# Partial sums added in memory by transfers, roundings held on ScalarE, a half chunk's work moved: an attention and two-FFN kernel

## The chip, the cores and the metric

The kernel runs on one core of one Trainium2 chip. The time is that of one execution on the device, in microseconds. The kernel before took 1273.68 us, the median of 3 runs (1272.46 to 1275.25). Engines are named as the profile does: PE is TensorE's matmuls, PEld its weight loads, DVE VectorE, ACT ScalarE, POOL GpSimd, SP SyncE, which here issues most transfers.

## The reference

```python
# x [8, 8, 512, 64], state [8, 8, 32, 64]
a     = softmax(scale * x @ state^T)          # tokens read the state
xread = a @ state
a2    = softmax(scale * state @ x^T)          # the state reads the tokens
sread = a2 @ x
x = concat([xread, sread], axis=2)            # -> [4352, 512]: 8 x (512 + 32) rows
x = relu(x @ w_in) ** 2 @ w_out               # w_in [512, 2048], w_out [2048, 512]
out = ((x @ w1) * (x @ w2) @ w3) @ w_out2     # w1, w2 [512, 1024], w3 [1024, 1024], w_out2 [1024, 512]
```

All in float32.

## The kernel before

Tokens are worked in nine chunks: chunks 0 to 7 are the 512 token rows of each batch, and chunk 8 (`B` in the code) holds the 256 rows of all state reads; it is called the half chunk here. A float32 matmul is done in three passes of a rounded part and a rest: `split` (lines 80 to 85) rounds a tile on ScalarE (line 84) and takes the rest by a subtraction on VectorE (line 85).

**First phase** (to 674.9 us): attention and the first FFN. Chunks 0, 1 and 2 start before all weights are converted, so their FFN sums are closed in parts: three for chunks 0 and 1, two for chunk 2. Each part is a tensor `y_scr[c][i]` in memory of its own. Beside this, `conv` converts the weights of the second FFN from their 64-bit form: the loads are three conversions ahead, VectorE works on a tile, and `make_later` stores it (line 221), with loads and stores on GpSimd's queue. 40 such tiles follow one another, one in every second step from step 32 on.

**Weight product** (674.9 to 723.6): w3 @ w_out2 is made once, in eight rows of matmuls into two PSUM banks `h` (`w34_rows`). From each pair of rows VectorE makes four sums, which are rounded and stored in `w34_sums` (lines 735 to 744).

**Two sweeps.** Sweep s = 0, 1 covers one half of the 1024 inner columns. A sweep begins with the half chunk: `load9`, `make9` (its roundings `y9q`), four `ab9`, two `out9`. Then come four pairs of chunks, (3,4), (5,6), (7,2), (0,1), in the second sweep in reverse order. For a pair, four `quad`s multiply a pair of token blocks with blocks of w1 and w2, in seven products of a 2 x 2 scheme in place of eight, and multiply the results; `out_pair`, the output stage, multiplies these with the weight product in seven products of the same scheme. The next pair's token blocks are loaded at the first quad (`load_pair`), and `make_pair` gives the jobs that round them and their differences; `out_pair` runs these between its products by `do(n)`.

`load_pair` loads the first part of a chunk's rows, and for a chunk with more parts loads each of these and adds it on GpSimd (lines 801 to 804).

In the first sweep the output stage stores its result in scratch memory (`oscr`). In the second sweep `fetch` loads this, and `put` adds it on GpSimd (line 1079) before a store to `out` (line 1082). The last pair of all (`ends`) takes the loaded tile up in VectorE's add from PSUM (line 1064).

**Order.** A planner places the instructions of a program on each engine's queue by their dependences, so an instruction may go ahead of others that stand before it in the code. `tc.issue_after(ins)` holds the instructions of a block behind `ins` on `ins`'s own engine. In `out_pair`, `last` is a VectorE instruction of the last quad, so it holds VectorE's part of the jobs only:

```python
def do(n):
    with tc.issue_after(last.ins):
        for job in jobs[:n]:
            job()
```

Tiles of one tag share that tag's buffers; a tile waits until the earlier user of its buffer is through, transfers included. Tags in play: `s0` (2 buffers) to `s3` for the quads' copies from PSUM (line 898), `r` (2, in `pa`) and `qc` (2) for `q0`, `qb` for `q1`, `yo` for stores. The pool `bp` opens after the weight product's pool `w34p` has closed, on its memory, and each of its tiles waits only for the tiles that it lies on.

Of the kernel before, what the change touches and what calls it, by code (L numbers as in the profile page):

```python
# [8 lines left out]
F32 = mybir.dt.float32  # L9
# [11 lines left out]
def kernel(  # L21
# [37 lines left out]
    def f32(ap):  # L59
        return ap.bitcast(F32)  # L60
# [139 lines left out]

    turned = range(N1, N1 + 2 * N1)

    def load_later(i):
# [506 lines left out]
    w34_sums = [dram.tile([P, 4, 2, NH], F32, name=f"w34u{i}") for i in range(2 * NB)]  # L710
    even = []

    def w34_rows(kk):
        ps = bank_h("ps_w34")
        for j in range(N1):
# [18 lines left out]
        d = pa.tile([P, 512], F32, tag="r", bufs=2, name="d34").rearrange("p (i n) -> p i n", i=2)  # L734
        for n, (i, in0, in1, op) in enumerate((
            (0, v[:, 1], e[:, 1], ALU.add), (1, d[:, 0], e[:, 0], ALU.subtract),
            (0, v[:, 0], d[:, 1], ALU.subtract), (1, e[:, 0], e[:, 1], ALU.subtract),
        )):
            if n % 2 == 0:
                q = pa.tile([P, 2, 2, NH], F32R, tag="ghl", bufs=3, name="u34")  # L740
            nc.vector.tensor_tensor(out=d[:, i], in0=in0, in1=in1, op=op)
            split(q[:, n % 2, HI], q[:, n % 2, LO], d[:, i])
            if n % 2:
                nc.sync.dma_start(w34_sums[u][:, n - 1:n + 1], f32(q))
        if u >= NB:
            nc.sync.dma_start(w34_s[u - NB], f32(w34_t[u]))


# [137 lines left out]
    def quad(c0, c1, m):  # L886
# [41 lines left out]

    def load9():
# [77 lines left out]
    OUTS = {"11": (0, 0), "12": (1, 0), "21": (0, 1), "22": (1, 1)}  # L1007
    IN_AT = {
        ("11", 0): "r", ("11", 1): "r", ("12", 0): "qd", ("12", 1): "qb",
        ("22", 0): "qb", ("22", 1): "qc", ("21", 0): "qc", ("21", 1): "r",  # L1010
    }
    AT = {"11": ("s0", "s1"), "22": ("yo", "yo"), "12": ("s0", "s2"), "21": ("s0", "s3")}
    TWO = ("s0", "yo", "r", "qb", "qc")
# [4 lines left out]

    def out_pair(c0, c1, s, jobs, last, ends, more):
# [32 lines left out]

        def fetch(block, kept=False):
            if s == 1 and kept == ends:
                for tp in range(2):
                    t = o_in[block, tp] = place(AT[block][tp] if kept else IN_AT[block, tp], "opart")
                    nc.sync.dma_start(t, scr(*where(block), tp))

# [12 lines left out]
        def put(block, ts, ps):  # L1071
            c, i = where(block)
            for tp, t in enumerate(ts):
                nc.vector.tensor_tensor(out=t, in0=ps[tp], in1=t, op=ALU.add)  # L1074
                if s == 0:
                    nc.sync.dma_start(scr(c, i, tp), t)
                    continue
                if not ends:
                    nc.gpsimd.tensor_tensor(out=t, in0=t, in1=o_in.pop((block, tp)), op=ALU.add)  # L1079
                rows_t = "(p j) e -> p j e" if c < BLK else "(j p) e -> p j e"  # L1080
                dst = out[c * T:c * T + S, i * NH:(i + 1) * NH].rearrange(rows_t, j=J)
                nc.sync.dma_start(dst[:, 2 * tp:2 * tp + 2], t.rearrange("p (j e) -> p j e", j=2))

        for block in ("11", "22", "12"):
            fetch(block, True)
        bA = [bank_h("oa") for _ in range(2)]
# [7 lines left out]
        late(1)  # L1094
        fetch("11")
        product(bD, "S4", "B22", first=False)
        load_turn(s, 3)
        late(2)
        fetch("12")
        do(1)  # L1100
# [3 lines left out]
        late(3)  # L1104
        fetch("22")
        fetch("21")
# [3 lines left out]
        put("12", t12, bD)  # L1110
        fetch("21", True)
        do(1)
# [3 lines left out]
        if more:  # L1116
            load_turn(s, 2)
        bC = [bank_y(2 + d, "oc") for d in range(2)]
# [21 lines left out]

    pairs = [(3, 4), (5, 6), (7, 2), (0, 1)]
    raw9 = load9()
    raw = load_pair(*pairs[0])
    make9(raw9)
    for job in make_pair(raw):
        job()
    for s, todo in enumerate((pairs, pairs[::-1])):
        if s == 1:
            make9(raw9)
            for t in range(NT9 // P):  # L1150
                load_o9(t)
# [4 lines left out]
        load_sums(s)  # L1156
        load_turn(s, 2)
        for i, (c0, c1) in enumerate(todo):
# [13 lines left out]
            out_pair(c0, c1, s, jobs, last, s == 1 and not more, more)  # L1172
            if s == 0 and i + 1 == len(todo):
                raw9 = left.pop("y9")
                for j in range(NB):
# [31 lines left out]
```

## Time and profile before

| | |
|---|---|
| median of 3 runs | 1273.68 us |
| profiled execution | 1271.22 us, its span 1269.1 us |
| PE busy | 1226.6 us, 97% of the span |
| PEld busy | 1006.5 us, 79% |
| DVE busy | 901.1 us, 71% |
| ACT busy | 669.2 us, 53% |
| POOL busy | 140.1 us, 11% |
| mean granted TensorE clock | 0.984 of 2.4 GHz |
| GpSimd's adds of parts, line 804 | 24, 33.0 us |
| GpSimd's adds of outputs, line 1079 | 24, 36.5 us |

The span is from the first to the last instruction; what is over is before and after. Busy shares are means over stages that differ, so the reader needs the waits and timelines of single places beside them. A releaser in a row is the instruction that ended an engine's wait.

### The profile page before, as it was taken

To read this page: it belongs to the slowest core of one execution; us is meant where nothing else is said; L and a number is where in the kernel's file an instruction comes from. 1 tells how busy PE (TensorE), PEld (TensorE's weight loads), DVE (VectorE), ACT (ScalarE), POOL (GpSimd) and SP (SyncE) were. 2 spreads that over 40 slices of the span, in tenths; PEclk is the share of its full clock that TensorE was granted. 3 is DMA by queue.
4 is the path that set the end of the run, shared out by engine and by line. 5 is a ranking of instruction groups with operands and counts; after the bars stand their busy time and mean duration, and the time that the engine had idled before them with its cause. 6 is when DMAs were issued, how large, how long until landed. Compare 5 with 4: busy or idle time off the path is not lost. (4 is left out here: it accounts for less than half of the span.)

```text
span 1269.1 us, 19143 instructions
## 1 busy us (share of the span) xinstructions
PE 1226.6 (97%) x7184; PEld 1006.5 (79%) x7184; DVE 901.1 (71%) x1590; ACT 669.2 (53%) x1221; POOL 140.1 (11%) x182
## 2 busy tenths in 40 slices
PE   7999999999999999999999799999799899999998
PEld 5677777777777777777898698898689788888878
DVE  6977877676775757532448737888687669797877
ACT  6876556564554646454656535454445334444532
POOL 0000010232321011000000000102400012021210
PEclk9999999999999999999999999999899999999989
DMA  7445664646445353012325540606241714243314
GB/s 232 137 163 176 145 193 126 162 143 126 126 102 164 109 150 124 27 43 53 106 76 172 186 140 1 200 17 207 76 166 44 250 56 140 93 133 100 132 52 133
DMA packets 134620, 158.01 MB, mean 125 GB/s; under 512 B 73344, under 2 KB 85120, under 8 KB 134016
## 3 DMA queue, kind: packets, MB, share of 16 engines
q1 hardware_dynamic: 124800, 125.34, 32.6%
q0 software_dynamic: 9728, 31.47, 8.0%
q8 instruction: 56, 0.92, 0.3%
q14 instruction: 36, 0.29, 0.1%
HBM read 106.95 MB, written 49.81 MB: 124 GB/s over the span
## 5 line engine op out<-in xcount | busy, mean ns | idle before, releaser
L501 PE MATMUL y<-ghl,wo 128*128 128x512 f32 (+1 forms) x1728 | 403.1, 381 | 0.8 <-ACT ghl L84 0.4
L501 PEld LDWEIGHTS y<-ghl,wo 128*128 128x128 f32 x1728 | 309.4, 188 | 87.9 <-ACT r L449 15.1
L85 DVE TENSOR_TENSOR ghl<-r,ghl 128x512 fp32r<-128x512 f32 (+1 forms) x144 | 94.8, 658 | 161.1 <-ACT ghl L84 158.1
L890 PE MATMUL qa<-yq,wq 128*128 128x512 f32 x576 | 148.4, 399 | 9.8 <-ACT s L898 9.8
L890 PEld LDWEIGHTS qa<-yq,wq 128*128 128x128 f32 x576 | 110.5, 193 | 34.3 <-ACT s L898 11.4
L898 ACT COPY s<-qa 128x512 f32<-128x512 f32 x96 | 56.5, 588 | 141.0 <-PE qa L890 119.8
L85 DVE TENSOR_TENSOR z<-q,z 128x512 fp32r<-128x512 f32 x112 | 81.6, 751 | 28.3 <-ACT z L84 28.0
L890 PE MATMUL qd<-yq,wq 128*128 128x512 f32 x384 | 99.3, 395 | 1.1 <-ACT s L898 1.1
L84 ACT CAST yq<-yraw 128x512 fp32r<-128x512 f32 x98 | 59.4, 621 | 60.7 <-DVE yraw L819 43.1
L451 ACT ACTIVATE r<-r 128x512 f32<-128x512 f32 (+1 forms) x144 | 87.8, 610 | 3.3
L84 ACT CAST ghl<-r 128x512 fp32r<-128x512 f32 (+1 forms) x144 | 86.2, 599 | 3.6
L84 ACT CAST z<-q 128x512 fp32r<-128x512 f32 x112 | 68.5, 621 | 37.0 <-DVE q L920 11.6
L890 PEld LDWEIGHTS qd<-yq,wq 128*128 128x128 f32 x384 | 73.7, 192 | 17.2 <-ACT s L898 1.5
L804 POOL TENSOR_TENSOR yraw<-yraw,yp 128x512 f32<-128x512 f32 x24 | 33.0, 1378 | 457.6 <-DVE q L926 278.7
L85 DVE TENSOR_TENSOR yq<-yraw,yq 128x512 fp32r<-128x512 f32 x98 | 70.8, 747 | 3.7 <-ACT yq L84 3.6
L902 DVE TENSOR_TENSOR s<-qa,s 128x512 f32<-128x512 f32 x32 | 22.1, 691 | 61.7 <-ACT s L898 61.7
L890 PE MATMUL qe<-yq,wq 128*128 128x512 f32 x192 | 52.9, 414 | 4.5 <-DVE o L1074 4.5
L1079 POOL TENSOR_TENSOR o<-o,opart 128x512 f32<-128x512 f32 x24 | 36.5, 1540 | 145.0 <-DVE o L1074 91.1
L890 PE MATMUL qc<-yq,wq 128*128 128x512 f32 x192 | 48.7, 389 | 0.0
L890 PEld LDWEIGHTS qe<-yq,wq 128*128 128x128 f32 x192 | 38.1, 200 | 13.3 <-DVE o L1074 5.4
L844 DVE TENSOR_TENSOR q<-q,q 128x512 f32<-128x512 f32 x64 | 47.4, 751 | 0.1
L819 DVE TENSOR_TENSOR yraw<-yraw 128x512 f32<-128x512 f32 x56 | 44.9, 837 | 2.7 <-DMA yraw<-yscr 2.7
(592 smaller groups left out, 2105.3 us busy)
## 6 DMA issues: line engine op xcount, KB each, us to landing
yraw<-yscr SPq DMA_DIRECT2D x56, 256.0 KB, 5.2
yscr<-yo SPq DMA_DIRECT2D x52, 256.0 KB, 2.7
oscr<-o SPq DMA_DIRECT2D x34, 256.0 KB, 2.2
opart<-oscr SPq DMA_DIRECT2D x34, 256.0 KB, 3.1
raw<-in_moe_w_out_dram SPq DMA_DIRECT2D x16, 512.0 KB, 4.4
raw<-in_moe_w_dram POOLq DMA_DIRECT2D x64, 128.0 KB, 3.4
raw<-in_moe_w_dram POOLq DMA_DIRECT2D x16, 512.0 KB, 4.7
raw<-in_moe_w_in_dram SPq DMA_DIRECT2D x12, 512.0 KB, 3.8
```

The lines of the kernel that those rows point to most:

```text
L84: nc.scalar.copy(hi, src)
L85: return nc.vector.tensor_tensor(out=lo, in0=src, in1=f32(hi), op=ALU.subtract)
L451: nc.scalar.activation(r[:, :n], r[:, :n], ACTF.Square)
L501: nc.tensor.matmul(y_ps[c, d][:, :n], wo_t[f][:, wi, d * P:(d + 1) * P], t[:, gi, :n], start=(f == f0 and k == 0), stop=(f == f1 - 1 and k ...
L804: nc.gpsimd.tensor_tensor(out=t[:, n], in0=t[:, n], in1=p, op=ALU.add)
L819: nc.vector.tensor_tensor(out=out(kt), in0=a(kt), in1=b(kt), op=ALU.subtract)
L844: return nc.vector.tensor_tensor(out=t, in0=a, in1=b, op=ALU.subtract)
L890: nc.tensor.matmul(ps, W[w, kt][:, wi, m * P:(m + 1) * P], Y[v, kt][:, vi, :], start=(first and kt == 0 and k == 0), stop=(last and kt == ...
L898: nc.scalar.copy(t, ps)
L902: nc.vector.tensor_tensor(out=t, in0=ps, in1=t, op=ALU.add)
L1079: nc.gpsimd.tensor_tensor(out=t, in0=t, in1=o_in.pop((block, tp)), op=ALU.add)
```

## The change

Five edits. (1) Five transfers of 1 MB on GpSimd's queue, behind five of the last thirteen stores of converted weights, add the parts of chunks 0, 1 and 2 into `y_scr[c][0]` in memory; `load_pair` loads only that. (2) Except for the pair that is first in the first sweep and last in the second, the first sweep stores its outputs in `out`, and the second adds to them there by accumulating transfers on GpSimd's queue; the tiles of blocks 12 and 21 take other tags. (3) The jobs of `out_pair` are also held behind the last copy of the last quad on ScalarE. (4) The half chunk's tiles are loaded under `s0` and `qb` in `bp`; for the second sweep its roundings are a job ahead of the later weights. (5) The weight sums are made in another order, two reads of PSUM first, and the rest after the next row of matmuls is begun.

```diff
+    parts = [(c, part) for c in range(BLK) for part in y_scr[c][1:]]
...
-        nc.gpsimd.dma_start(later[i][0], w)
+        store = nc.gpsimd.dma_start(later[i][0], w)
+        if i >= len(later) - 13 and (len(later) - 1 - i) % 3 == 0:
+            c, part = parts.pop(0)
+            with tc.issue_after(store.ins):
+                nc.gpsimd.dma_start(y_scr[c][0], part, accum_op=ALU.add, max_dma_last_dim=512)
...
     def w34_rows(kk):
+        while rest:
+            rest.pop()()
...
-        for n, (i, in0, in1, op) in enumerate((
-            (0, v[:, 1], e[:, 1], ALU.add), (1, d[:, 0], e[:, 0], ALU.subtract),
-            (0, v[:, 0], d[:, 1], ALU.subtract), (1, e[:, 0], e[:, 1], ALU.subtract),
-        )):
...
+        nc.vector.tensor_tensor(out=d[:, 0], in0=v[:, 1], in1=e[:, 1], op=ALU.add)
+        nc.vector.tensor_tensor(out=d[:, 1], in0=v[:, 0], in1=e[:, 0], op=ALU.add)
...
+        def sums():
+            for n, (i, in0, in1) in enumerate((
+                (0, None, None), (1, d[:, 1], d[:, 0]), (1, e[:, 0], e[:, 1]), (0, d[:, 0], e[:, 0]),
+            )):
...
+        rest.append(sums)
...
                 nc.sync.dma_start(t[:, n], y_scr[c][0][:, d, :])
-                for part in y_scr[c][1:]:
-                    p = pa.tile([P, 512], F32, tag="yo", bufs=2, name="yp")
-                    nc.sync.dma_start(p, part[:, d, :])
-                    nc.gpsimd.tensor_tensor(out=t[:, n], in0=t[:, n], in1=p, op=ALU.add)
...
-            nc.scalar.copy(t, ps)
+            left["copy"] = nc.scalar.copy(t, ps)
...
-            t = pa.tile([P, 2, NT9], F32, tag="r", bufs=2, name="y9")
+            t = pool.tile([P, 2, NT9], F32, tag=tag, bufs=2, name="y9")
...
-            nc.sync.dma_start(f32(t), w34_sums[s * NB + i][:, 0:2])
+            nc.sync.dma_start(f32(t[:, 0]), w34_sums[s * NB + i][:, 0])
+            nc.sync.dma_start(f32(t[:, 1]), w34_sums[s * NB + i][:, 3])
...
-    AT = {"11": ("s0", "s1"), "22": ("yo", "yo"), "12": ("s0", "s2"), "21": ("s0", "s3")}
+    AT = {"11": ("s0", "s1"), "22": ("yo", "yo"), "12": ("r", "r"), "21": ("qc", "qc")}
...
-        jobs = list(jobs)
+        ends = s == 1 and not more
+        jobs, gate = list(jobs), left["copy"]
...
-            with tc.issue_after(last.ins):
+            with tc.issue_after(last.ins), tc.issue_after(gate.ins):
...
+            for tp in range(2) if ends else ():
+                t = o_in[block, tp] = place(AT[block][tp], "opart")
+                nc.sync.dma_start(t, scr(*where(block), tp))
...
-                if s == 0:
+                if s == 0 and first:
                     nc.sync.dma_start(scr(c, i, tp), t)
                     continue
-                if not ends:
-                    nc.gpsimd.tensor_tensor(out=t, in0=t, in1=o_in.pop((block, tp)), op=ALU.add)
...
+                if s == 0 or ends:
+                    nc.sync.dma_start(dst, src)
+                else:
+                    nc.gpsimd.dma_start(dst, src, accum_op=ALU.add)
...
-    raw9 = load9()
+    raw9 = load9(bp, "s0")
     raw = load_pair(*pairs[0])
     make9(raw9)
+    while rest:
+        rest.pop()()
...
         if s == 1:
-            make9(raw9)
...
-                jobs.insert(3, lambda: left.__setitem__("y9", load9()))
+                jobs[3:4] = [lambda: make9(left.pop("y9")), jobs[3]]
+                jobs.insert(2, lambda: left.__setitem__("y9", load9(bp, "qb")))
```

In the last pair of all, block 12 is now fetched after the second group of late roundings and block 21 after block 11's adds; before, 12 was fetched at the stage's start and 21 after block 12's adds.

## Rows read from the trace of the kernel before

**Rows 1.** The waits of TensorE: engine, line, releaser: us in total, times, longest.

```profile
PE qa L890 <- ACT s L898: 9.8, 4, 5.6
PE ab L951 <- ACT y9q L84: 6.0, 1, 6.0
...
PE qe L890 <- DVE o L1074: 4.5, 3, 1.6
PE ab L951 <- DVE y9q L85: 4.4, 2, 4.0
...
PE ps_w L718 <- DVE d L741: 1.7, 1, 1.7
```

**Rows 2.** Sums by stretch: length, busy us (instructions) of each engine, PEclk, DMA.

```profile
784.33:804.48 20.15, 20.15 (x169) 20.14 (x168) 19.33 (x33) 11.64 (x21) 0.00 (x0) 1.00 0.23 77
...
784.33:842.59 58.26, 58.26 (x337) 51.69 (x336) 48.17 (x76) 29.46 (x52) 5.43 (x4) 1.00 0.33 109
842.59:909.36 66.77, 60.09 (x338) 52.48 (x337) 52.75 (x76) 28.94 (x51) 21.65 (x16) 0.97 0.47 142
909.36:968.86 59.50, 59.50 (x338) 52.93 (x336) 46.55 (x76) 30.59 (x55) 0.39 (x1) 0.98 0.25 89
...
1050.27:1114.94 64.67, 61.80 (x337) 53.69 (x336) 53.50 (x76) 29.19 (x52) 12.19 (x8) 0.95 0.35 114
...
1179.72:1244.54 64.82, 61.94 (x337) 53.74 (x336) 53.44 (x76) 25.97 (x46) 12.14 (x8) 0.95 0.28 94
```

**Rows 3.** Sums by stretch where the granted clock is low, around both `ab` stages.

```profile
727.87:734.69 6.82, 5.09 (x23) 5.06 (x24) 4.53 (x9) 3.81 (x9) 0.00 (x0) 0.50 0.56 190
...
997.52:1000.93 3.41, 3.08 (x16) 2.79 (x15) 2.15 (x5) 0.10 (x1) 0.00 (x0) 0.50 0.64 202
```

**Rows 4.** Timeline, second sweep's first boundary: start, us, what, [idle before <-releaser].

```profile
1064.56 3.00 POOL L1079 TENSOR_TENSOR o<-o,opart 128x512 f32<-128x512 f32 x2 [34.95 <-DVE o L1074]
...
1064.94 3.16 DVE L85 TENSOR_TENSOR z<-q,z 128x512 fp32r<-128x512 f32 x2
...
1076.93 2.93 PE L890 MATMUL qe<-yq,wq 128*128 128x512 f32 x6 [1.58 <-DVE o L1074]
```

**Rows 5.** Timeline of VectorE at the first sweep's first boundary.

```profile
785.15 0.69 DVE L902 TENSOR_TENSOR s<-qa,s 128x512 f32<-128x512 f32 x1 [2.27 <-ACT s L898]
...
797.80 1.28 DVE L1074 TENSOR_TENSOR o<-oe,o 128x512 f32<-128x512 f32 x2
799.00 1.28 DVE L85 TENSOR_TENSOR z<-q,z 128x512 fp32r<-128x512 f32 x2
...
806.22 1.27 DVE L1074 TENSOR_TENSOR o<-oc,o 128x512 f32<-128x512 f32 x2
```

**Rows 6.** Timeline of ScalarE before pair (0, 1), first sweep.

```profile
905.48 0.62 ACT L84 CAST yq<-yraw 128x512 fp32r<-128x512 f32 x1 [6.47 <-POOL yraw L804]
```

**Rows 7.** DMA issues: tile, queue, count, KB each, median us to landing.

```profile
opart<-oscr SPq DMA_DIRECT2D x34, 256.0 KB, 3.1
...
w12s<-cw POOLq DMA_DIRECT2D x16, 256.0 KB, 2.3
...
w34b<-w34s SPq DMA_DIRECT2D x2, 1024.0 KB, 7.2
```

**Rows 8.** GpSimd's stores of line 221: ns min/median/max, first and last start.

```profile
L221 POOL DMA_DIRECT2D w12s<-cw x16: 539/546/552, 400.1 to 538.4; - x16
```

**Rows 9.** Timeline of ScalarE and TensorE as the first sweep's next quads begin.

```profile
807.43 0.59 ACT L898 COPY s<-qd 128x512 f32<-128x512 f32 x1 [0.56 <-PE qd L890]
...
807.46 1.52 PE L890 MATMUL qe<-yq,wq 128*128 128x512 f32 x6
...
809.95 1.52 PE L890 MATMUL qd<-yq,wq 128*128 128x512 f32 x6
```

**Rows 10.** Sums of tile yq's instructions (PE, PEld, DVE, ACT), last quad.

```profile
774.80:784.33 9.53, 9.53 (x43) 7.70 (x41) 0.00 (x0) 3.54 (x6) 1.00 0.01 2
```

**Rows 11.** Timeline of ScalarE before the first `ab`.

```profile
729.14 0.71 ACT L84 CAST y9q<-y 128x256 fp32r<-128x256 f32 x2 [0.24 <-DMA y<-yscr]
```

More of the change, by code (lines that the diff above doesn't have):

```diff
@@ L710 @@
     w34_sums = [dram.tile([P, 4, 2, NH], F32, name=f"w34u{i}") for i in range(2 * NB)]
-    even = []
+    even, rest = [], []
     def w34_rows(kk):
+        while rest:
+            rest.pop()()
         ps = bank_h("ps_w34")
@@ L734, in w34_rows @@
         d = pa.tile([P, 512], F32, tag="r", bufs=2, name="d34").rearrange("p (i n) -> p i n", i=2)
-        for n, (i, in0, in1, op) in enumerate((
-            (0, v[:, 1], e[:, 1], ALU.add), (1, d[:, 0], e[:, 0], ALU.subtract),
-            (0, v[:, 0], d[:, 1], ALU.subtract), (1, e[:, 0], e[:, 1], ALU.subtract),
-        )):
[L739 to L744, printed above, removed]
+        nc.vector.tensor_tensor(out=d[:, 0], in0=v[:, 1], in1=e[:, 1], op=ALU.add)
+        nc.vector.tensor_tensor(out=d[:, 1], in0=v[:, 0], in1=e[:, 0], op=ALU.add)
         if u >= NB:
             nc.sync.dma_start(w34_s[u - NB], f32(w34_t[u]))
+        def sums():
+            for n, (i, in0, in1) in enumerate((
+                (0, None, None), (1, d[:, 1], d[:, 0]), (1, e[:, 0], e[:, 1]), (0, d[:, 0], e[:, 0]),
+            )):
+                if n % 2 == 0:
+                    q = pa.tile([P, 2, 2, NH], F32R, tag="ghl", bufs=3, name="u34")
+                if in0 is not None:
+                    nc.vector.tensor_tensor(out=d[:, i], in0=in0, in1=in1, op=ALU.subtract)
+                split(q[:, n % 2, HI], q[:, n % 2, LO], d[:, i])
+                if n % 2:
+                    nc.sync.dma_start(w34_sums[u][:, n - 1:n + 1], f32(q))
+        rest.append(sums)
     QM = N1 // 2
@@ L927, in quad, with load9 @@
         return to_z(m, q0, q1)
-    def load9():
+    def load9(pool, tag):
         ts = []
         for h in range(2):
-            t = pa.tile([P, 2, NT9], F32, tag="r", bufs=2, name="y9")
+            t = pool.tile([P, 2, NT9], F32, tag=tag, bufs=2, name="y9")
             nc.sync.dma_start(t, y_scr[B][0][:, 2 * h:2 * h + 2, :])
@@ L1017, in place, with out_pair @@
         return pool.tile([P, 512], F32, tag=tag, bufs=2 if tag in TWO else 1, name=name)
-    def out_pair(c0, c1, s, jobs, last, ends, more):
-        jobs = list(jobs)
+    def out_pair(c0, c1, s, jobs, last, first, more):
+        ends = s == 1 and not more
+        jobs, gate = list(jobs), left["copy"]
         def do(n):
-            with tc.issue_after(last.ins):
+            with tc.issue_after(last.ins), tc.issue_after(gate.ins):
                 for job in jobs[:n]:
@@ L1051, in where, with fetch @@
             return (c0, c1)[k], i
[L1053 to L1057, printed above, removed]
+        def fetch(block):
+            for tp in range(2) if ends else ():
+                t = o_in[block, tp] = place(AT[block][tp], "opart")
+                nc.sync.dma_start(t, scr(*where(block), tp))
         def keep(block, ps):
@@ L1074, in put @@
                 nc.vector.tensor_tensor(out=t, in0=ps[tp], in1=t, op=ALU.add)
-                if s == 0:
+                if s == 0 and first:
                     nc.sync.dma_start(scr(c, i, tp), t)
                     continue
-                if not ends:
-                    nc.gpsimd.tensor_tensor(out=t, in0=t, in1=o_in.pop((block, tp)), op=ALU.add)
                 rows_t = "(p j) e -> p j e" if c < BLK else "(j p) e -> p j e"
[L1081 to L1085, printed above, removed]
+                dst = out[c * T:c * T + S, i * NH:(i + 1) * NH].rearrange(rows_t, j=J)[:, 2 * tp:2 * tp + 2]
+                src = t.rearrange("p (j e) -> p j e", j=2)
+                if s == 0 or ends:
+                    nc.sync.dma_start(dst, src)
+                else:
+                    nc.gpsimd.dma_start(dst, src, accum_op=ALU.add)
+        for block in ("11", "22"):
+            fetch(block)
         bA = [bank_h("oa") for _ in range(2)]
@@ L1094, in out_pair @@
         late(1)
-        fetch("11")
+        fetch("12")
         product(bD, "S4", "B22", first=False)
-        load_turn(s, 3)
+        load_turn(s, 2)
         late(2)
-        fetch("12")
         do(1)
@@ L1104, in out_pair @@
         late(3)
-        fetch("22")
         fetch("21")
@@ L1110, in out_pair @@
         put("12", t12, bD)
-        fetch("21", True)
         do(1)
@@ L1116, in out_pair @@
         if more:
-            load_turn(s, 2)
+            load_turn(s, 1)
         bC = [bank_y(2 + d, "oc") for d in range(2)]
@@ L1156 @@
         load_sums(s)
-        load_turn(s, 2)
+        load_turn(s, 1)
         for i, (c0, c1) in enumerate(todo):
@@ L1169 @@
                 jobs = make_w(raw)
-                jobs.insert(3, lambda: left.__setitem__("y9", load9()))
+                jobs[3:4] = [lambda: make9(left.pop("y9")), jobs[3]]
+                jobs.insert(2, lambda: left.__setitem__("y9", load9(bp, "qb")))
             more = i + 1 < len(todo)
-            out_pair(c0, c1, s, jobs, last, s == 1 and not more, more)
+            out_pair(c0, c1, s, jobs, last, i == 0, more)
             if s == 0 and i + 1 == len(todo):
-                raw9 = left.pop("y9")
                 for j in range(NB):
```

4 lines of the change are left out of this document (removed).

## The prediction, made before the changed kernel was run

> **What bounds the kernel now.** I read the page's busy shares first: TensorE is busy for 97% of the span, so time can come only from its idle stretches and from stretches at the lower of its two clock levels. The list of TensorE's waits came next [rows 1]: 9.8 us before `qa` for copies of ScalarE, 6.0 and 4.4 us before `ab` for the half chunk's roundings, 4.5 us before `qe` for VectorE's output adds, 1.7 us before `ps_w`. That is 26.4 us, all of it in code that the change touches.
>
> The idle time is not the whole price. The sums by stretch [rows 2] go from the first matmul of one output stage to that of the next, one period of pairs. An undisturbed period is 58.26 us: an output stage of 20.15 and four quads in 38.11, 9.5 each, TensorE busy throughout at clock 1.00. The period that ends before pair (0, 1)'s output takes 66.77 us in its place, the next one 59.50. The second sweep's three take 64.67 to 64.82 (first and last shown, the middle one is 64.78) at a mean clock of 0.95. Where TensorE has just stood still, the granted clock is 0.50 for some microseconds, 1.2 instead of 2.4 GHz [rows 3]: 6.82 us around the first `ab`, 3.41 around the second. Half of TensorE's busy time in such a stretch is loss.
>
> The timelines say why TensorE waited. At the second sweep's boundary [rows 4], GpSimd adds two tiles in 3.00 us, and two VectorE subtractions beside them take 3.16 us; the same two take 1.28 us in the first sweep [rows 5]. There VectorE runs on from 785.15 to 807.49 without a gap, and its read of bank 2 (the first of the last two adds) ends at 806.9, 0.5 us before TensorE's `qe` starts to write there [rows 9]. VectorE and TensorE bound this stage together, so what GpSimd takes from VectorE comes out as idle time before `qe`. In the last quad before pair (0, 1), a rounding waits 6.47 us for GpSimd's adds, and the copy that TensorE needs is queued behind it [rows 6].
>
> **The change, part by part.**
>
> *No adds on GpSimd in the second sweep.* VectorE then has the work that it has in the first sweep, so each period should be 58.26: a gain of 6.41 to 6.56, three times, 19.5 us. In place of the adds and of SP's stores stand eight accumulating transfers per pair, for three pairs, on GpSimd's queue. Each waits for its VectorE add, and behind it stand only the next ones. The trace has no accumulating transfer. Bounds for one of 256 KB: 2.3 us, a GpSimd store, and 5.4, that store after a load of 3.1 [rows 7]. I take 4, in the middle, since the added read may overlap the write. The first to wait for it is the tile of tag `s1`: its VectorE add ends at 799.08 [rows 5], the next quad's copy into it starts at 807.43, and TensorE needs that copy at 809.95 [rows 9], 10.9 us after the add. Two transfers one after the other with an issue of 0.55 [rows 8] take 8.6 us, or 11.4 at the upper bound: cost 0, at most 0.5 per boundary. Blocks 12 and 21 move to tags `r` and `qc`, first needed again at the end of the next pair's first and second quad, one or two times 9.5 us later; off the path. SP loses loads and stores that nothing waits for after this.
>
> GpSimd's 16 stores of one kind all issue in 0.539 to 0.552 us [rows 8]. The Trainium skill ("SBUF — State Buffer", section "SBUF: two separate sides") speaks against this part: VectorE in its two-port modes keeps GpSimd from writing descriptors, and it gives 620 ns that became 3100 ns. By that, two issues and two transfers would take 14.2 us and some 3.3 us would be lost at each of three boundaries; the sum goes by the rows.
>
> The Trainium skill ("Collectives: The Full Stack", section "The bandwidth ceiling: the fold count and why AG ≠ RS ≠ AR") says that an add inside the DMA engines needs two reads per write and runs at about half of a copy's rate. By that the upper bound is the likelier one, and the sum loses 1.5 us; no row here shows it.
>
> *Parts of chunks added in memory.* Five transfers of 1 MB, each issued behind a store, every third one; the stores are 9.2 us apart (16 from 400.1 to 538.4 [rows 8]), so one comes each 27.7 us. Bounds for one: 2.3 us, that of the quarter size, and 14.4, twice a 1 MB load of 7.2 [rows 7]. I take 10, nearer to the two passes. The loads queued behind it are three conversions ahead of their use, 27.7 us again, and that cover hides it; without it the excess over 27.7 us would stall VectorE's conversions. Cost 0. What goes are the loads of parts, GpSimd's adds and the rounding's wait for them, so the periods of 66.77 and 59.50 fall to 58.26 each: 9.75 us.
>
> *ScalarE's roundings held.* Six casts, 3.54 us, now run in the quad before the output stage [rows 10]. Held behind that quad's last copy they join 11.64 us of ScalarE's work in the stage of 20.15 [rows 2], 15.2 in all. There is room, but VectorE's subtractions wait for these casts, and VectorE has 0.5 us to spare. So each of six boundaries (three per sweep) loses between 0, if the casts fall into ScalarE's gaps, and 3.5, if none does. I take 0.5, near the lower end, since the stage leaves 8.5 us free on ScalarE: 3.0 us lost. A gain I exclude: what these casts delayed was one copy behind GpSimd's adds, and that is counted above.
>
> *Half chunk first.* In sweep 0 its load waits for the `r` tiles of the weight sums, and ScalarE's rounding for the load [rows 11]. The new tile `s0` is the first of a pool that replaces staging tiles read long before, so its two loads can move on SP's queue past the last stores of sums, and the roundings ahead of the last weight rows' end. Gain 6.0 [rows 1] plus half of 5.09 [rows 3], 8.5; bounds 0, if the tile lies on one in use until the last matmul, and 8.5. I take 7.5, because VectorE is crowded there. In sweep 1 the subtractions stand in VectorE's queue behind the new weights' sums; as a job ahead of these they are done before the output stage ends. Gain 4.4 [rows 1] plus half of 3.08 [rows 3], 5.9. Late next would be the halves of A21 and A22, which follow them at once in that queue.
>
> *Weight sums deferred.* The bank comes free after two reads in a row, no longer with splits between them: 1.7 us [rows 1]. One subtraction more for each of four groups, about 0.3 us (half of 0.64, for half the width [rows 5]), runs beside matmuls. Four loads of sums per sweep in place of two have the four quads to land in; 0.
>
> *The last pair.* Its fetches of blocks 12 and 21 move to other tiles, each still ahead of its use. I take 0, and as ends the smallest wait of [rows 1], 1.7 either way.
>
> Sum: 19.5 + 9.75 + 7.5 + 5.9 + 1.7 - 3.0 = 41.4 us. The profiled execution took 1271.22 us (its span 1269.1 and 2.1 around it), so 1229.8 on its own scale. The median of the runs shown lies 2.5 above it; on that scale the forecast is 1232.
>
> **Rivals.** *The half chunk's tile comes late.* The pool's first place may not be what I think; the 7.5 us stay: 1239.5. For: the trace shows no addresses. Against: the older pool's first tiles are the staging tiles.
>
> *VectorE stays late.* Something else lengthens the second sweep's boundary (the issues on GpSimd, say), and its whole loss stays, 19.5 us: 1251. For: 0.5 us to spare. Against: the two subtractions at 3.16 us beside GpSimd's adds and at 1.28 without.
>
> *ScalarE becomes the bound.* The held casts make VectorE some 3 us late at six boundaries and the clock falls each time as now: 6 × 6.4 = 38, less the 3 counted, 1267. For: VectorE's row without a gap. Against: 8.5 us free on ScalarE.
>
> *Slower: accumulating transfers fall behind.* With T per 256 KB, `s1` comes late beyond T = 5.2 (2T + 0.55 = 10.9); beyond 7.3, eight don't fit into 58.26 us; the 1 MB ones, at 4T, exceed 27.7 us beyond 6.9. At T = 9 the last two cost 3 × (72 - 58.3) + 4 × (36 - 27.7) = 74 us: 1306. At about T = 7.7 the gain is gone: 10 and 12 us in these places and some 19 for `s1` with the low clock. For: no row shows such a transfer. Against: the bounds from rows end at 5.4.
>
> **How the numbers follow.** The forecast has 0.62 (its own range 1226 to 1238), the half chunk's tile 0.12, VectorE 0.10, ScalarE 0.06, the slow transfers 0.08, no change at all 0.02. Faster by over 0.2%, about what a measurement of this kernel can tell: the first four, 0.90; same 0.02; slower 0.08. The range starts at 1223 (nothing lost to the held casts, all 8.5 of the half chunk, the last pair's 1.7, and 3 for the scale, whose runs differ by that) and ends at 1251, with VectorE's rival.
>
> **What would show it.** TensorE's waits before `qa`, `qe`, `ab` and `ps_w` gone or under 1 us each; periods of second-sweep pairs of 58 to 59 us at clock 1.00; no VectorE subtraction of 1.5 us in them; accumulating transfers that land in 3 to 5 us; a first phase as long as before. Wrong would be: idle time before `qe` with VectorE waiting for ScalarE's casts, a copy into `s1` that waits for a transfer, or conversions that wait for loads on GpSimd's queue.

## The result: 45 us faster, and the profile after

| | before | after |
|---|---|---|
| median of the runs | 1273.95 us (4 runs, 1272.46 to 1275.25) | 1228.9 us (4 runs, 1228.23 to 1229.14) |
| profiled execution, its span | 1271.22, 1269.1 us | 1229.14, 1227.3 us |
| TensorE busy share, mean granted clock | 97%, 0.984 | 99%, 0.997 |

The ratio of the medians is 0.9646, with an interval of 0.9629 to 0.9663. The forecast was 1232 us (1223 to 1251); the time lies 3.1 us below it.

The profile's page after: span, busy time (share) and instructions of each engine.

```profile
span 1227.3 us, 18920 instructions
...
PE 1209.5 (99%) x7184; PEld 996.9 (81%) x7184; DVE 871.0 (71%) x1594; ACT 665.9 (54%) x1221; POOL 109.5 (9%) x163
```

The waits of TensorE after, in the columns of [rows 1]. In this execution no line of the output stages, of the quads, of `ab` or of `ps_w` is left; what remains is in the start of the kernel or under 1.2 us.

```profile
PE ps_x L294 <- DVE X L247: 5.6, 1, 5.6
PE ps_sw L438 <- ACT xT L299: 1.9, 1, 1.9
PE ps_x L294 <- ACT X L245: 1.5, 1, 1.5
PE ps_a L362 <- DVE e L352: 1.1, 2, 0.9
...
```

A second profile of the same kernel (run 11) does have a wait before `ab`, and its stretch from the first `ps_w` to the first output stage (columns of [rows 2]) is longer than the 99.00 us below:

```profile
PE ab L961 <- ACT y9q L84: 1.1, 1, 1.1
```

```profile
676.88:777.40 100.52, 99.21 (x482) 83.41 (x481) 71.40 (x137) 48.60 (x97) 0.00 (x0) 1.00 0.44 149
```

Sums by stretch after, in the columns of [rows 2] and [rows 3]: an output stage, one of the first sweep's periods, the first and last of the second sweep's, the phase before the weight product, the stretch from the first `ps_w` to the first output stage, the one from the first sweep's last output stage to the second's first, the end, and a stretch of the start at the low clock.

```profile
777.28:797.43 20.15, 20.15 (x169) 20.15 (x168) 19.33 (x33) 14.49 (x27) 0.00 (x0) 1.00 0.23 79
...
835.54:893.80 58.26, 58.26 (x337) 51.69 (x336) 46.48 (x76) 28.88 (x52) 0.00 (x0) 1.00 0.28 91
...
1027.30:1085.56 58.26, 58.26 (x337) 51.69 (x336) 46.48 (x76) 28.88 (x52) 9.58 (x8) 1.00 0.42 91
...
1143.82:1202.08 58.26, 58.26 (x338) 51.69 (x336) 46.48 (x76) 28.88 (x52) 9.52 (x8) 1.00 0.36 69
...
0.00:678.28 678.28, 665.41 (x4065) 515.31 (x4065) 448.15 (x879) 404.69 (x737) 80.83 (x139) 0.99 0.50 134
678.28:777.28 99.00, 98.89 (x482) 83.53 (x481) 71.28 (x137) 48.85 (x97) 0.00 (x0) 1.00 0.44 151
952.06:1027.30 75.24, 75.24 (x457) 67.71 (x456) 53.86 (x92) 33.87 (x66) 0.00 (x0) 1.00 0.42 133
1202.08:1227.30 25.22, 20.41 (x169) 20.15 (x167) 18.86 (x31) 5.23 (x9) 0.00 (x0) 1.00 0.47 157
29.66:36.49 6.83, 6.83 (x25) 4.39 (x22) 5.25 (x17) 4.81 (x11) 0.00 (x0) 0.50 0.02 8
```

Every period is now the undisturbed 58.26 us, in both sweeps, with TensorE busy throughout at clock 1.00. The held casts are in the output stage (ScalarE 14.49 us in it, before 11.64).

The same stretches of the trace before, for the two that [rows 2] doesn't have:

```profile
674.90:784.33 109.43, 101.74 (x482) 85.57 (x481) 70.58 (x133) 52.11 (x103) 0.00 (x0) 0.97 0.41 137
968.86:1050.27 81.41, 77.04 (x457) 68.88 (x456) 55.92 (x92) 33.88 (x64) 5.52 (x4) 0.98 0.41 136
```

So the spans' difference of 41.8 us divides as follows.

| stretch | before | after | gain | forecast |
|---|---|---|---|---|
| start to the first `ps_w` | 674.90 | 678.28 | -3.38 | 0 |
| to the first output stage | 109.43 | 99.00 | 10.43 | 9.2 (7.5 + 1.7) |
| first-sweep periods (all but the first's 58.26) | 126.27 | 116.52 | 9.75 | 9.75 |
| to the second sweep's first output stage | 81.41 | 75.24 | 6.17 | 5.9 |
| second-sweep periods | 194.27 | 174.78 | 19.49 | 19.5 |
| from the last output stage to the end | 24.56 | 25.22 | -0.66 | 0 |
| held roundings, in all of these | | | not seen | -3.0 |

In run 11's profile the second row's stretch is 100.52, a gain of 8.9: this row differs by 1.5 us between two executions of the changed kernel. The nine other runs below that leave this stretch's matmuls and weight sums as they are (all but 5 and 6) have 99.28 to 99.90. The loss in the first row lies ahead of the first matmul into `y`. By the view of that line (count, ns min/median/max, first and last start; before, then after) it starts at 35.3 and at 38.8 us:

```profile
L501 PE MATMUL y<-ghl,wo x1728: 278/389/504, 35.3 to 674.8; 128*128 128x512 f32 x171, 128*128 128x256 f32 x21
```

```profile
L506 PE MATMUL y<-ghl,wo x1728: 278/389/505, 38.8 to 678.2; 128*128 128x512 f32 x171, 128*128 128x256 f32 x21
```

From there to the first `ps_w` it is 639.6 us before and 639.5 after. The five transfers of 1 MB are issued in that part, from 433 to 542 us, and TensorE lost nothing by them.

VectorE's timeline at the second sweep's first boundary (start, length, what), to be held against [rows 4] and [rows 5]: the two subtractions beside it take 1.28 us again.

```profile
1040.77 1.28 DVE L1081 TENSOR_TENSOR o<-oe,o 128x512 f32<-128x512 f32 x2
1041.97 1.28 DVE L85 TENSOR_TENSOR z<-q,z 128x512 fp32r<-128x512 f32 x2
```

There GpSimd issues two transfers in a row; the copy into `s1` that must wait for the second is ScalarE's, and `qe` follows without a wait, as in [rows 9].

```profile
1041.75 2.44 POOL L1091 DMA_DIRECT2D out_dram<-o  x2 [497.44 <-DVE o L1081]
```

```profile
1050.40 0.59 ACT L908 COPY s<-qd 128x512 f32<-128x512 f32 x1 [0.77 <-PE qd L900]
```

```profile
1050.43 1.52 PE L900 MATMUL qe<-yq,wq 128*128 128x512 f32 x6
```

The DMA list after, in the columns of [rows 7], and the issues' row (count, then total and mean ns of one, then idle time), against [rows 8]:

```profile
out_dram<-o POOLq DMA_DIRECT2D x24, 256.0 KB, 6.2
...
yscr<-yscr POOLq DMA_DIRECT2D x5, 1024.0 KB, 10.6
```

```profile
L1091 POOL DMA_DIRECT2D out_dram<-o x24 | 28.6, 1597 | 597.3 <-DVE o L1081 597.2 <-issue 0.2
```

The 6.2 us are a median over 24 issues, and most of these stood behind others in the queue. The first two at this boundary, by the view of their tensor (ns of the issues, their starts, and us from issue to landing):

```profile
L1091 POOL DMA_DIRECT2D out_dram<-o x2: 1227/1460/1692, 1041.8 to 1042.5; - x2
...
DMA to landing us min/median/max: 4.0/5.8/7.6
```

The first, with none ahead of it, landed 4.0 us after its issue (4.1 at each of the other two boundaries), as the T = 4 of the prediction. The second, that of `s1`, landed at 1050.11, 7.6 us after its own issue and 8.36 after the first one (7.5 and 7.6 at the others). That is 0.3 us before the copy above, which TensorE's matmul released and not the transfer. The first issue took GpSimd 1.2 us, where 0.55 was taken; the mean of 1.6 counts issues that ran beside others. Nothing waits for any of them.

### The profile page after: what moved, and what is told of

Read it like the earlier page. It is cut to its first block, busy times and chain, and to the rows that moved or that the text cites. A ratio compares the mean times of both kernels' runs of the same rounds, so it can differ in the third digit from the quotient of the medians.

```text
span 1227.3 us, 18920 instructions
## 1 busy us (share of the span) xinstructions
PE 1209.5 (99%) x7184; PEld 996.9 (81%) x7184; DVE 871.0 (71%) x1594; ACT 665.9 (54%) x1221; POOL 109.5 (9%) x163
## 4 chain that ended last, share of the span: by engine, by line
PE 92%; DMA 3%; DVE 2%; ACT 1%; SPq 1%; issue 0%; DVEq 0%; ACTq 0%
PE y L506 30%; PE qa L900 10%; PE qd L900 7%; PE oa L1051 6%; PE od L1051 4%; PE qc L900 4%; PE qe L900 4%; PE ps_sw L438 3%; PE ab L961 2%; PE oe L1051 2%; PE oc L1051 2%; DMA yraw<-yscr 1%; PE po L991 1%; DMA x<-in_x_dram 1%; PE ps_w L725 1%; PE ps_s L307 1%
## 5 line engine op out<-in xcount | busy, mean ns | idle before, releaser
L900 PE MATMUL qa<-yq,wq 128*128 128x512 f32 x576 | 143.7, 389 | 0.0
L900 PEld LDWEIGHTS qa<-yq,wq 128*128 128x128 f32 x576 | 107.7, 188 | 22.0
L85 DVE TENSOR_TENSOR z<-q,z 128x512 fp32r<-128x512 f32 x112 | 74.1, 685 | 23.8 <-ACT z L84 23.7
L1091 POOL DMA_DIRECT2D out_dram<-o x24 | 28.6, 1597 | 597.3 <-DVE o L1081 597.2
L85 DVE TENSOR_TENSOR yq<-yraw,yq 128x512 fp32r<-128x512 f32 x98 | 64.3, 682 | 3.3 <-ACT yq L84 3.2
L900 PE MATMUL qe<-yq,wq 128*128 128x512 f32 x192 | 48.7, 389 | 0.0
L85 DVE TENSOR_TENSOR sw<-ps_sw,sw 128x512 fp32r<-128x512 f32 (+1 forms) x66 | 42.1, 667 | 2.8 <-ACT sw L84 2.6
L725 PE MATMUL ps_w<-wo,w3T 128*128 128x512 f32 x192 | 43.7, 389 | 0.0
L854 DVE TENSOR_TENSOR q<-q,q 128x512 f32<-128x512 f32 x64 | 43.0, 682 | 0.0
L900 PEld LDWEIGHTS qc<-yq,wq 128*128 128x128 f32 x192 | 36.0, 188 | 7.5
```

What stands on the lines that cost most here:

```text
L85: return nc.vector.tensor_tensor(out=lo, in0=src, in1=f32(hi), op=ALU.subtract)
L725: nc.tensor.matmul(ps, t[:, wi, (j % 4) * P:(j % 4 + 1) * P], wo2_t[j][:, vi, :], start=(j == 0 and k == 0), stop=(j == N1 - 1 and k == 2),)
L854: return nc.vector.tensor_tensor(out=t, in0=a, in1=b, op=ALU.subtract)
L900: nc.tensor.matmul(ps, W[w, kt][:, wi, m * P:(m + 1) * P], Y[v, kt][:, vi, :], start=(first and kt == 0 and k == 0), stop=(last and kt == ...
L1091: nc.gpsimd.dma_start(dst, src, accum_op=ALU.add)
```

## The experiments

Each kernel is the changed one with one edit. "The changed kernel" is 1228.9 us; a second series of it, run beside the later experiments, gave 1230.08.

**1. The hold taken back.**

```diff
-            with tc.issue_after(last.ins), tc.issue_after(gate.ins):
+            with tc.issue_after(last.ins):
```

> The changed kernel with the hold on ScalarE's roundings taken back, all else kept. If the parts added in memory alone ended the wait before pair (0, 1), the hold is worth nothing either way: 1229 us (1227 to 1231), no TensorE wait above 0.5 us after the first phase. If the hold was needed (casts that run ahead make the quads' copies late at every boundary), waits before qa return, 1 to 6 us at up to six boundaries: 1235 to 1260.

1228.06 us (1227.68 to 1228.49), ratio 0.9646 as with the hold. Its second first-sweep period, in the same columns:

```profile
834.66:892.92 58.26, 58.26 (x337) 51.69 (x336) 46.50 (x76) 29.41 (x52) 0.00 (x0) 1.00 0.28 91
```

In the changed kernel the hold costs nothing and gives nothing. My 3.0 us for it are not there.

**2. The second sweep's outputs fetched and added by GpSimd again.**

```diff
+                if not ends:
+                    nc.gpsimd.tensor_tensor(out=t, in0=t, in1=o_in.pop((block, tp)), op=ALU.add)
...
-                    nc.gpsimd.dma_start(dst, src, accum_op=ALU.add)
...
+                nc.sync.dma_start(dst, src)
```

The fetches, tiles and stores of before come back with it.

> The changed kernel with the second sweep's outputs fetched and added on GpSimd again, with the tiles of before; all else kept. If GpSimd's adds (by VectorE's slowing and the late tiles) were the cause, the three second-sweep periods are 64 to 65 us again and the clock falls at each: 1229 + 19.5 = 1248 us. If VectorE's lateness there had another cause, which the other edits removed, the periods stay at 58 to 60: under 1236.

1248.82 us, 19.9 above the changed kernel. The waits of TensorE, VectorE's subtractions and a period's sums are back to [rows 1], [rows 4] and [rows 2]:

```profile
PE qe L900 <- DVE o L1086: 4.4, 3, 1.6
PE qa L900 <- ACT s L908: 4.2, 3, 1.6
```

```profile
1042.26 3.18 DVE L85 TENSOR_TENSOR z<-q,z 128x512 fp32r<-128x512 f32 x2
```

```profile
1027.59:1092.31 64.72, 61.85 (x337) 53.71 (x336) 53.48 (x76) 28.69 (x52) 12.19 (x8) 0.95 0.35 115
```

This part alone is worth the 19.5 us of the forecast, within the spread of the runs.

**3 and 4. The parts of chunks added by GpSimd again, with the hold and without it.** Both drop the five transfers (not shown) and put back, behind each load of a pair:

```diff
+                for part in y_scr[c][1:]:
+                    p = pa.tile([P, 512], F32, tag="yo", bufs=2, name="yp")
+                    nc.sync.dma_start(p, part[:, d, :])
+                    nc.gpsimd.tensor_tensor(out=t[:, n], in0=t[:, n], in1=p, op=ALU.add)
```

> The changed kernel with the parts of chunks loaded and added on GpSimd again, the hold kept. If the cost of these adds was that a rounding stood in ScalarE's queue ahead of the copy that TensorE needs, the hold alone cures most of it: the period before pair (0, 1) is 58 to 62 us, 1229 to 1233 in all. If it was that the sums come late or slow VectorE, the loss returns whole: 66 to 67 us for that period, 1238 to 1240.

> As the run before, and the hold taken back too. Both theories expect the kernel before at this place: 66.8 us for the period before pair (0, 1), 59.5 for the next, 1229 + 9.75 = 1239 us. If it is under 1233, the wait before pair (0, 1) was removed by another of the edits.

1234.07 us with the hold, 1241.37 without. The first lies between the two ranges expected for it, so neither theory alone holds; the second is 2.4 us above the 1239 expected. The periods before pair (0, 1)'s output, with the hold and without it (columns of [rows 2]):

```profile
892.02:955.77 63.75, 60.19 (x337) 53.19 (x336) 49.01 (x76) 28.90 (x52) 6.99 (x6) 0.97 0.30 99
```

```profile
835.61:903.91 68.30, 61.68 (x337) 53.58 (x336) 52.38 (x76) 29.09 (x51) 21.84 (x16) 0.94 0.46 139
```

ScalarE's timeline just before and in pair (0, 1)'s output stage, without the hold: the rounding that waits for GpSimd stands ahead of the copy into `s`, as in [rows 6].

```profile
900.03 0.62 ACT L84 CAST yq<-yraw 128x512 fp32r<-128x512 f32 x1 [6.76 <-POOL yraw L814]
900.55 0.58 ACT L908 COPY s<-qa 128x512 f32<-128x512 f32 x1
```

With the hold a wait of 3.94 us for GpSimd falls into the output stage, ahead of a copy out of a bank that TensorE waits for before the product `od`. So the hold cures the part of the loss before `qa` and leaves the late sums.

```profile
898.79 0.62 ACT L84 CAST yq<-yraw 128x512 fp32r<-128x512 f32 x1 [3.94 <-POOL yraw L814]
899.31 0.58 ACT L1074 COPY o<-oa 128x512 f32<-128x512 f32 x1
```

```profile
PE od L1051 <- ACT o L1074: 3.6, 1, 3.6
```

Runs 1, 3 and 4 and the changed kernel make a table of two by two: 1228.9 and 1228.06 with the transfers, 1234.07 and 1241.37 with GpSimd's adds. The hold is worth 7.3 us where the adds are on GpSimd, and nothing once they are in memory; the transfers are worth 5.2 us with the hold and 13.3 without it.

**5. The half chunk back in its old place,** in both sweeps (the weight sums' last group still made before it).

```diff
-    raw9 = load9(bp, "s0")
+    while rest:
+        rest.pop()()
+    raw9 = load9(pa, "r")
...
         if s == 1:
+            make9(left.pop("y9"))
...
-                jobs[3:4] = [lambda: make9(left.pop("y9")), jobs[3]]
```

> The changed kernel with the half chunk's edit taken back in both sweeps: its first load into the tiles of the weight sums again (these sums made ahead of it, since they share the tiles), its second rounding after the first sweep's last output stage. If both waits were the load's and the queue's place, 6 to 7 us before the first ab and 4 to 5 before the second return with the low clock: 1229 + 14.4 = 1243 us (1240 to 1246). If the deferred weight sums had cured the first wait by themselves, only the second returns: 1235.

1246.11 us, 17.2 above the changed kernel and just over the 1240 to 1246 expected. By stretch it is 108.65 in place of 99.00 us before the first output stage and 82.23 in place of 75.24 in the transition, 16.6 together. TensorE's waits:

```profile
PE ab L961 <- ACT y9q L84: 8.3, 1, 8.3
...
PE ab L961 <- DVE y9q L85: 4.0, 1, 4.0
```

The first wait is longer than the 6.0 of [rows 1], and the record doesn't show why; so this run shows the cause, and its price for it may be too high.

**6. The weight sums made at once,** with splits between the two reads of the bank, in the old order and with the old loads of sums.

```diff
...
+            nc.vector.tensor_tensor(out=d[:, i], in0=in0, in1=in1, op=op)
+            split(q[:, n % 2, HI], q[:, n % 2, LO], d[:, i])
...
-        rest.append(sums)
```

> The changed kernel with the weight sums made in the old order, at once. If the bank's late release costs what it did, TensorE waits 1.7 us before ps_w again: 1230.7 us. If the half chunk's earlier load has emptied VectorE's queue there, or the bank was late for a load, no wait above 0.5: 1229. If the half chunk's roundings then stand behind the sums, more than 3 us: over 1232.

1230.59 us (1229.77 to 1233.1), 1.7 above the first series of the changed kernel and 0.5 above the second, so the time alone doesn't tell. The waits say more: 2.0 us before `ps_w`, where the changed kernel has none in its first profile and 0.2 in its second. A further 0.9 us before `ab` tells nothing, since run 11 has 1.1 there.

```profile
PE ps_w L725 <- DVE d L748: 2.0, 2, 1.3
```

By stretch it is 102.54 us from the first `ps_w` to the first output stage, against 99.00 and 100.52; the profiled execution is the slowest of the four.

```profile
678.34:780.88 102.54, 99.59 (x482) 83.33 (x481) 69.90 (x133) 48.57 (x97) 0.00 (x0) 1.00 0.43 146
```

**7. Plain stores in place of the accumulating ones.** It leaves out the sum with the first sweep's outputs.

```diff
-                    nc.gpsimd.dma_start(dst, src, accum_op=ALU.add)
+                    nc.gpsimd.dma_start(dst, src)
```

> The changed kernel with plain stores from GpSimd's queue in place of the second sweep's accumulating transfers; it leaves out the sum with the first sweep's outputs. If the accumulating transfers are hidden, the same time: 1229 (1227 to 1231), with landings of 2 to 3 us against 6.2. If they cost something that shows as no wait of TensorE (slower loads, a later end), 1 to 4 us less: 1225 to 1228.

1230.41 us (1229.23 to 1232.31): the accumulation, with its longer landing, costs nothing that a measurement tells. The two rows as above, from the DMA list and the issues:

```profile
out_dram<-o POOLq DMA_DIRECT2D x24, 256.0 KB, 2.8
```

```profile
L1091 POOL DMA_DIRECT2D out_dram<-o x24 | 17.1, 717 | 607.6 <-DVE o L1081 606.7 <-DMA w34b<-w34u 0.9
```

**8. An idle add on GpSimd behind each accumulating transfer,** whose result nothing reads.

```diff
+                    dummy = bp.tile([P, 512], F32, tag="dummy", bufs=1, name="dummy")
+                    nc.gpsimd.tensor_tensor(out=dummy, in0=t, in1=t, op=ALU.add)
```

> The changed kernel with one idle addition on GpSimd behind each accumulating transfer of the second sweep (it reads the output tile and writes a tile that nobody uses): GpSimd's adds without their loads and without their place in the outputs' way. If GpSimd's reading slows VectorE and that made qe wait, VectorE's subtractions take 1.4 to 1.8 us beside it and each of the three periods is 2 to 6.5 us longer: 1235 to 1248. If the outputs' late landing was the cause, the periods stay within 1 us of 58.26: 1229 to 1232.

1263.67 us (1259.75 to 1264.09), 34.8 above the changed kernel and more than either theory gave. VectorE's subtractions beside these adds, and two of the waits that follow:

```profile
1045.24 1.92 POOL L1093 TENSOR_TENSOR dummy<-o 128x512 f32<-128x512 f32 x1
...
1046.04 3.91 DVE L85 TENSOR_TENSOR yq<-yraw,yq 128x512 fp32r<-128x512 f32 x2
```

```profile
PE qe L900 <- DVE o L1081: 12.4, 3, 4.8
PE qc L900 <- DVE yq L85: 6.3, 3, 2.4
```

The adds also hold up the transfers behind them, and a copy waits for one of these:

```profile
1048.11 0.58 ACT L908 COPY s<-qd 128x512 f32<-128x512 f32 x1 [1.10 <-DMA out_dram<-o]
```

But TensorE's `qe` starts only at 1051.80, released by VectorE's adds, and VectorE had worked up to these without a gap; so the late landing isn't what binds there. It is GpSimd's arithmetic beside VectorE that costs the time, not the fetches and stores that went with it. It costs more here than in the kernel before. One difference shows in the timeline: these adds stand between the issues on GpSimd's queue, and so run on into the next quad. Whether that is the whole surplus wasn't tried.

**9 and 12. Slower accumulating transfers.** Each tile in two transfers, of pieces of 256 and of 128 bytes.

```diff
+                    for j in range(2):
+                        nc.gpsimd.dma_start(dst[:, j], src[:, j], accum_op=ALU.add, max_dma_last_dim=256)
```

> The changed kernel with each accumulating transfer of the second sweep cut into two, and their rows of 1 KB into pieces of 256 B: four times as many pieces. If only the tile s1 limits how slow they may be (10.9 us from its add to TensorE's need), an issue of 1.6 us that grows about fourfold brings its landing to some 14 us: a copy into s1 waits for the transfer, TensorE stands still 2 to 4 us at three boundaries and the clock falls: 1240 to 1252. If the issue hardly grows with the pieces, no wait: 1229 to 1231.

> As the run with pieces of 256 B, now of 128 B: eight times the changed kernel's count. There the copy into s1 waited 1.5 us for its transfer and TensorE's 2.5 us of tolerance covered it. If s1 is the limit, its transfer lands some 5 us later still, TensorE stands still 2 to 5 us at each of three boundaries, more where the queue runs on into the next quads, and the clock falls: 1240 to 1260, with the wait of ScalarE's copy s for out_dram ahead of TensorE's. If the pieces are not what sets the landing, no wait: 1229 to 1231.

The diff is run 9's; run 12 has 128 in the place of 256. 1229.73 us (1227.55 to 1230.36) and 1229.87 (1229.33 to 1231.53): two misses. The transfers became slower and TensorE hardly waited. With pieces of 128 bytes GpSimd issues for 25 us of each period, and the DMA engines are busy for 0.78 to 0.86 of it. The first period is 58.30 us, the others 58.59 and 58.50:

```profile
1026.46:1084.76 58.30, 58.30 (x338) 51.69 (x336) 46.48 (x76) 28.68 (x52) 25.04 (x16) 1.00 0.85 91
```

Something does wait for the transfers. In run 9 it is the copy into `s1`:

```profile
1051.87 0.59 ACT L908 COPY s<-qd 128x512 f32<-128x512 f32 x1 [1.53 <-DMA out_dram<-o]
```

In run 12 VectorE waits for them too (total, times, longest):

```profile
DVE q L936 <- DMA out_dram<-o: 6.4, 2, 3.3
```

TensorE needs that copy 2.5 us after it can start, and that took up the lateness of run 9. Even in run 12 the second half of the `s1` tile landed 9.9 to 10.2 us after the first issue, inside the slack of 10.9, so the slack itself was not crossed. The three periods of run 12 are 0.6 us over 3 x 58.26 in all; where accumulating transfers begin to cost more stays open.

**10 and 11. The start of the kernel filled, and the changed kernel again beside it.** The account by stretch leaves a start that takes 3.4 us more in the profile after. Sixteen matmuls of the identity, whose result nothing reads, go into TensorE's 1.9 us wait before `ps_sw`.

```diff
...
+    def fill():
+        t = bank_y(0, "fill")
+        with tc.issue_after(last_x[-1].ins):
+            for _ in range(16):
+                nc.tensor.matmul(t[:, :P], ident, ident, start=True, stop=True)
...
```

> The changed kernel with 16 idle matmuls of the identity in the 1.9 us in which TensorE waits at 27 to 29 us of the span. If that idle time (with the shorter ones before it) lets the clock fall from 29.7 to 36.5 us, this stretch stays at full clock and the median falls by 2 to 3.4 us against the changed kernel of the same call. If the clock's fall at the start hangs on the time before, or the matmuls come in the way of the first FFN tiles: the same, or up to 1 us more.

> The changed kernel again, for the comparison with the run before in the same call: 1228.9 us, and in its profile the first phase between 674.9 and 678.3 us, as the clock at the start falls out.

1227.72 us with the fill (5 runs, 1226.75 to 1228.79), 1230.08 without (4 runs, 1229.34 to 1231.41), on the same chip: 2.4 us, and the two ranges don't overlap. The filled kernel's ratio is 0.9638 (0.9622 to 0.9655); that of run 11 is 0.9658 (0.9641 to 0.9675) and of the changed kernel's first series 0.9646, so the intervals of the ratios overlap. The stretch from 20 to 45 us (columns of [rows 2]) with the fill, then again of the changed kernel:

```profile
20.00:45.00 25.00, 22.27 (x151) 17.05 (x152) 23.63 (x58) 20.94 (x40) 0.00 (x0) 1.00 0.39 123
```

```profile
20.00:45.00 25.00, 22.02 (x116) 14.11 (x116) 21.92 (x54) 19.84 (x39) 0.00 (x0) 0.93 0.35 112
```

The clock fits the gain, but the other profiles speak for caution. Run 1's has 1.00 in this stretch without a fill, the first one of the changed kernel 0.86. Without a fill the first matmul into `y` started at 37.0 us in run 1 and at 36.2 in run 8, with it at 36.3. The start varies from execution to execution, so the pair of time ranges is the evidence and the clock is only the likely cause.

## Why the prediction was right, and where its sizes were off

*The second sweep (19.5 us forecast, 19.49 measured).* Right, and for the reason given: run 2 brings it back by GpSimd's adds, run 8 exceeds it by idle adds without the old fetches and stores. The Trainium skill ("SBUF — State Buffer", section "Who interferes with whom") says that a VectorE instruction with both inputs in SBUF contends with a GpSimd instruction that reads SBUF. The traces agree: in run 8 two pairs of subtractions beside GpSimd's adds took 3.15 and 3.91 us, where a pair takes 1.28 without adds. A third pair took 1.29 beside an add that itself took 2.82.

*The parts (9.75, measured 9.75).* The periods of 66.77 and 59.50 [rows 2] are 58.26. The 1 MB transfers landed in 10.6 us, 10 taken, and TensorE lost nothing in the part of the first phase in which they run. But it was not the only edit that could have brought much of this: with GpSimd's adds left in place, the hold is worth 7.3 us (runs 3 and 4). The two edits remove one wait, and a price for each alone would count the same microseconds twice. The prediction gave the hold no gain for that reason, and here it was right.

*The held roundings (-3.0 forecast, 0 measured).* This is the largest mis-sized term. The step that failed is that each boundary would lose 0.5 us because VectorE's subtractions wait for the casts. Run 1 has the same 58.26 without the hold. ScalarE's 2.85 us more in the output stage fall in its idle time, of which it had 8.5 us; the lower bound, none lost, was the right value.

*The half chunk (7.5 and 5.9 forecast).* Together with the weight sums' 1.7 the first stretch gave 10.43 in place of 9.2, and the transition 6.17. In run 11's execution the first stretch gave 8.9, and with the 99.28 to 99.90 of the other runs it would be 9.5 to 10.2. So this term was off by 1.2 us at most, and not always to one side: the profile after has no wait before `ab`, the others but run 5's still have 0.4 to 1.1 us there. Run 5, with 9.65 and 6.99 us for the undone edit, shows the cause, but does not fix the size. ScalarE's roundings are early:

```profile
724.36 1.35 ACT L84 CAST y9q<-y 128x256 fp32r<-128x256 f32 x4 [0.26 <-DMA y<-yscr]
```

against a start of 729.14 [rows 11], although the weight product begins 3.4 us later in this trace.

*The accumulating transfers (T = 4 us, bounds 2.3 to 5.4; 4.0 to 4.1 measured for one with none ahead).* The size was right for the term that the sum uses: `s1`'s transfer landed 7.5 to 8.4 us after the first issue, where 8.6 was forecast, inside the slack of 10.9. The sign "land in 3 to 5 us" was not met, with a median of 6.2, because I did not count the wait behind other transfers in it. Two parts were off: an issue took 1.2 us or more and not 0.55, and all eight of a boundary landed within 17.8 to 18.3 us of the first issue, 2.2 to 2.3 us each, so the later ones overlap and do not follow one another at T. The rival in which the transfers fall behind was not tested by runs 9 and 12. Run 12's last landings come up to 17.5 us after issue, but its eight tiles of a boundary land within 33.0 us, 4.1 each, where that rival needs 5.2 and more.

The Trainium skill ("Collectives: The Full Stack", section "The bandwidth ceiling: the fold count and why AG ≠ RS ≠ AR") puts an add inside the DMA engines at about half of a copy's rate. The traces agree in kind, with 4.0 to 4.1 us for an accumulating transfer with none ahead of it against 2.6 for the plain store of run 7; the 1.5 us that the prediction priced by it were not lost. The Trainium skill's stall of GpSimd's descriptors ("SBUF — State Buffer", section "SBUF: two separate sides"), cited in the prediction, was not seen: the issues took 1.17 to 2.65 us and no copy waited for them. The Trainium skill speaks there of VectorE in its two-port modes. Beside the issues of the second sweep's first boundary VectorE ran additions and subtractions of two inputs only, so they may not test that rule.

*The start and the scale (0 and 2.5 us).* The sign "a first phase as long as before" was not met: the phase is 3.38 us longer in the profile after, all of it ahead of the first matmul into `y`. The start of the profiled execution before was at full clock (1.00 from 20 to 45 us), that of the one after at 0.86. The clock goes with the loss but is not shown to be all of it: run 1's start, at 1.00, reached that matmul at 37.0 us. That the spans differ by 41.8 us, 0.4 from the forecast of 41.4, is luck. Leaving the first phase out, the traces give 45.2 us, and the medians 45.05. The forecast is short of that by 3.8: 3.0 for the hold, 1.5 for the half chunk's two stretches in this execution, less 0.66 lost at the end.

*The rivals.* The half chunk's tile came early: the stretch of 99.00 to 100.52 excludes a loss of the whole 7.5 us. VectorE was not late (no wait before `qe`) and ScalarE did not bound; the periods of 58.26 us exclude both.

## What to carry to other kernels

Move an addition out of an engine that shares time with the bound one first, and look at what it slows before what it takes: GpSimd worked 12.2 us in a period of 64.7 and cost 6.5 us of it through VectorE. Several edits for one wait are not additive: make them one by one and in pairs, as runs 1, 3 and 4 do, before each is given a price. Where a new operation's price is unknown, work out the slack of its first reader: here 10.9 us covered the 7.5 to 8.4 that the second transfer took. And ask of a median landing how many transfers stood ahead in the queue.

## What the runs showed of the hardware

- An accumulating transfer of 256 KB from SBUF, with none ahead of it, landed in 4.0 to 4.1 us and took GpSimd 1.17 to 1.23 us to issue (the plain store of run 7: 2.6 and 0.71 to 0.75). The median over all 24, with the wait behind others, is 6.2 (plain: 2.8). One of 1 MB between two places in memory landed in 10.6.
- The second of a group landed 3.4 to 4.3 us after the first, the later ones 0.7 to 2.8 us apart.
- Cut into smaller pieces, the issues grow: GpSimd issued for 9.5 us of a period with pieces of 1 KB, 20.7 at 256 bytes (run 9) and 25.0 at 128 (run 12), and the DMA share of the second sweep's first period went from 0.42 to 0.61 and 0.85. The periods grew by 0.33 us at most.
- GpSimd's additions beside VectorE's two-input subtractions made two of these take up to 3.91 us in place of 1.28, and three additions of VectorE 5.84 us, in run 8.
- The granted clock from 20 to 45 us was 0.86 in one execution of the changed kernel and 0.93 in another, and the first phase 678.28 and 676.88 us. Run 1, whose start is the same, had 1.00 and 676.82.
